# Decoding 64-bit weights: the low word and the sign taken from ScalarE to VectorE, with a new order of steps in the opening

## The chip, the cores and the metric

One core of a Trainium2 chip runs one program. The metric is the device time of that program in microseconds; a lower one is better. TensorE multiplies matrices, VectorE, ScalarE and GpSimd (POOL in the profile) work on elements, SyncE (SP) issues the transfers.

## The reference, cut to what matters

A windowed attention with a linear bias (8 batches, 8 heads, 576 positions, head size 64, window 128) is followed by a gated two-layer block:

```
scores = q k^T / 8 + slope * -(i - j)    where 0 <= i - j < 128
x      = softmax(scores) v                               # 576 x 512 per batch
h      = gelu(x w_in);  u, v = halves of h               # w_in 512 x 1024
v_n    = (v - mean) / sqrt(var + 1e-6) * g_ln
gated  = u * (w_sg v_n + b_sg)                           # w_sg 576 x 576
out    = x + gated w_out                                 # w_out 512 x 512
```

The scale factors that make `w_in` and `w_out` are 64-bit, so these two arrive as 64-bit floats.

## The kernel before

Every large product is made of three matmuls: each operand is split into a high and a low part of TensorE's short format, and high x high, high x low and low x high are added (`mm3`, line 570). The weights therefore have to be split before batch 0 can use them.

**Decode of one block of weights** (`split64`, lines 180 to 200; twelve blocks of 128 x 512: eight of `w_in`, k = 0 to 7, and four of `w_out`, k = 8 to 11; `add_wide`, line 500, makes the steps):
- `i{k}` loads the block into one of four buffers (SP, line 177).
- `d{k}` is three passes of ScalarE. L189 scales the low 32-bit word by 2^-29 and writes the rounded result as 16 bits into the low half of that word. L190 scales the high word by 2^-100 and writes it as a 16-bit float into the other half, so that only the sign is left. L191 writes the absolute value of the high word, rebased, to a temporary.
- `b{k}` shifts the temporary left by 3 bits (VectorE, L193). `+{k}` adds the low word to it as integers (GpSimd, L195). `H{k}` writes the high part (ScalarE, L197). `-{k}` writes the low part, the difference (L199; VectorE for odd k, GpSimd for even k).

**The other steps.** 32 pairs of heads, four per batch, each with: loads q and L; scores a and c, or * for both (TensorE, L252); score minima A, B, C, G with the bias (VectorE, L264 and L270); exponentials e, E, j, f, F (ScalarE, L280); R, the inverse of the sums (VectorE, L291, L292); scalings r, s, S (GpSimd, L296); transposes z, t, T (TensorE, L306, L319); masked copies X and Y (VectorE, L314, L315) and P (ScalarE); V, the values (TensorE, L337 to L345); x, h, k (ScalarE, L358 to L370) and l (GpSimd, L367), which gather the pair's output and split it. Per batch: v and tt (in batch 0 the v sums are cut into w and v steps), u, y and O with Oa are TensorE's sums; vg, tg, ug the gelu; nv..b, p, c, h and vn the normalisation of v (VectorE L594 to L602, GpSimd L599, ScalarE L607, VectorE L610), nt.. and tn the same for the tail of 64 rows, which ends in the tile vA; uc, gm, gh, gl, oa copies, gates and sums. wl, wH, w- and tl, tH, t-, bl, bH, b- load and split `w_sg` and the bias `b_sg`.

**Order.** Each step is registered with its engine, the steps that it follows and the buffers that it takes; the length given there is not used when the program is built. `ORDER`, a list written out by hand of all 1769 steps, is the order in which the steps are emitted; `pin` (line 873) makes the instructions of each engine keep that order, the SP queue too. So each engine works down its own part of the list and waits where a step that it needs has not ended. A y step of batch 0 needs all of vn, tn, w-, t- and b-; its last two matmuls (L722, L723) read vA and the tail of `w_sg`. A u step needs h and l of all four pairs and the low parts of blocks 4 to 7.

Of the kernel before, what the change touches and what calls it, by code (L numbers as in the profile page):

```python
# [908 lines left out]
```

## Time and profile before

| | |
|---|---|
| median of 3 runs | 605.91 us (605.49 to 606.16) |
| profiled execution, first to last instruction (span) | 603.9 us |
| TensorE busy (matmul) | 577.9 us, 96% |
| VectorE busy | 394.0 us, 65% |
| ScalarE busy | 374.9 us, 62% |
| GpSimd busy | 233.4 us, 39% |
| chain that ended last | TensorE 81%, ScalarE 10% of the span |

The table's shares are means over the whole span; the opening, in which the weights are decoded, has other limits than the rest. Of the profiled execution the span is its own time on record; the runs' median lies 2.0 us over it. L12 is line 12 of the kernel; a time in a timeline is counted from the span's start.

### The profile page before, as it was taken

The page shows a single profiled execution, that of the slowest core. Times are in us where ns is not written, and L with a number is a line of the kernel's source. Part 1 is how long each engine was busy: PE and PEld are TensorE (multiplying, and loading weights), DVE is VectorE, ACT ScalarE, POOL GpSimd, SP SyncE. Part 2 cuts the span into 40 slices and gives each one's busy share as a digit, 9 for nine tenths or more (in the row PEclk, how much of TensorE's full clock was granted, in tenths as well). Part 3 has the DMA queues.
Part 4 walks back from the last instruction along what each step waited for, and adds up shares of the span by engine and source line. Part 5 has one row for each costly group of instructions (what it writes and reads, how often), then busy time and mean ns, then how long its engine had stood idle before and what let it go on. Part 6 is the DMA issues. An engine that isn't in the chain of part 4 may idle for free.

```text
span 603.9 us, 16878 instructions
## 1 busy us (share of the span) xinstructions
PE 577.9 (96%) x6760; PEld 538.8 (89%) x6760; DVE 394.0 (65%) x1336; ACT 374.9 (62%) x1057; POOL 233.4 (39%) x248
## 2 busy tenths in 40 slices
...
GB/s 279 197 149 216 35 134 99 43 41 65 115 67 64 100 83 82 65 22 12 108 123 43 76 48 74 92 24 81 80 143 2 3 68 117 64 2 1 1 25 132
DMA packets 34898, 47.92 MB, mean 79 GB/s; under 512 B 2946, under 2 KB 24962, under 8 KB 34820
## 3 DMA queue, kind: packets, MB, share of 16 engines
...
q14 instruction: 25, 0.20, 0.1%
...
## 4 chain that ended last, share of the span: by engine, by line
PE 81%; ACT 10%; DVE 1%; POOL 1%; issue 1%; ACTq 0%
PE bank L574 20%; PE bank L576 20%; PE bank L575 20%; PE bank L252 5%; PE bank L337 5%; PE bank L306 4%; ACT e L280 3%; PE bank L342 2%; ACT wst L189 1%; PE bank L723 1%; PE bank L722 1%; PE bank L658 1%; PE bank L345 1%; PE bank L660 1%; ACT wst L190 1%
## 5 line engine op out<-in xcount | busy, mean ns | idle before, releaser
L280 ACT ACTIVATE e<-e,minima 128x128 f32<-128x128 f32 (+1 forms) x288 | 110.3, 385 | 15.0 <-DVE minima L264 14.5
L296 POOL TENSOR_TENSOR e<-e,rr 128x512 f32<-128x512 f32 (+1 forms) x96 | 75.7, 809 | 113.1 <-DVE rr L292 88.7
L264 DVE CUSTOM_DVE_ANT_0 e<-bank,bias 128x128 f32<-128x128 f32 (+1 forms) x320 | 75.9, 275 | 8.4 <-DVE bank L270 0.5
L599 POOL TENSOR_TENSOR rs<-rs,mhalf 128x1 f32<-128x1 f32 (+1 forms) x40 | 30.6, 769 | 126.1 <-DVE rs L596 126.0
L574 PE MATMUL bank<-ws,vn 128*128 128x288 f32 x256 | 78.0, 305 | 0.1
L574 PE MATMUL bank<-xs,wi 128*128 128x288 f32 x256 | 77.2, 302 | 0.7 <-ACT vg L648 0.7
L574 PE MATMUL bank<-g,wo 128*128 128x288 f32 x256 | 77.7, 303 | 0.0
L575 PE MATMUL bank<-xs,wi 128*128 128x288 f32 x256 | 75.5, 295 | 0.0
L576 PE MATMUL bank<-ws,vn 128*128 128x288 f32 x256 | 75.5, 295 | 0.0
L575 PE MATMUL bank<-g,wo 128*128 128x288 f32 x256 | 75.4, 295 | 0.0
L576 PE MATMUL bank<-g,wo 128*128 128x288 f32 x256 | 75.4, 295 | 0.0
L576 PE MATMUL bank<-xs,wi 128*128 128x288 f32 x256 | 75.4, 294 | 0.0
L575 PE MATMUL bank<-ws,vn 128*128 128x288 f32 x256 | 75.4, 294 | 0.0
L367 POOL TENSOR_TENSOR xs<-xf,xs 128x576 fp32r<-128x576 f32 x32 | 45.4, 1427 | 63.4 <-ACT xs L364 63.3
L270 DVE COPY_PREDICATED bank<-sel,bank 128x256 f32<-128x256 uint8 x128 | 54.0, 422 | 18.7 <-PE bank L252 17.7
L252 PE MATMUL bank<-qk 64*64 64x128 f32 (+2 forms) x1536 | 54.9, 287 | 5.6 <-DMA qk<-qkT 3.3
L314 DVE TENSOR_TENSOR px<-bank,m_own 128x512 f32<-128x512 f32 x64 | 43.7, 683 | 23.3 <-PE bank L306 12.6
L252 PEld LDWEIGHTS bank<-qk 64*64 64x64 f32 x1536 | 50.5, 141 | 8.8 <-DMA qk<-qkT 4.0
L737 POOL TENSOR_TENSOR g<-u,g 128x576 fp32r<-128x576 f32 x32 | 45.0, 1420 | 29.3 <-ACT g L734 29.1
L280 ACT ACTIVATION_READ_ACCUMULATOR e<-e,minima 128x1 f32 x288 | 54.3, 188 | 0.0
L574 PE MATMUL bank<-wi,xs 128*128 128x512 f32 x128 | 51.3, 401 | 2.1 <-DVE minima L264 2.1
L576 PE MATMUL bank<-wi,xs 128*128 128x512 f32 x128 | 50.4, 394 | 0.0
...
## 6 DMA issues: line engine op xcount, KB each, us to landing
...
wst<-w_in SPq DMA_DIRECT2D x8, 512.0 KB, 4.3
...
wst<-w_out SPq DMA_DIRECT2D x4, 512.0 KB, 3.2
...
```

Of the source, the lines that this page charges most:

```text
L252: return lambda: nc.tensor.matmul(banks[j][half[s ^ j], dst * R:(dst + k1 - k0) * R], qk[heads[j], 0, q * R:(q + 1) * R], qk[heads[j], 1, ...
L264: nc.vector.tensor_tensor_reduce(out=dst, in0=src, in1=bs, scale=-1.0 / math.sqrt(D), scalar=3e38, op0=ALU.add, op1=ALU.min, accum_out=acc)
L270: nc.vector.copy_predicated(sv[:, :, 0:P], sels[j][:, 0:2] if t2 == 0 else sels[j][:, 1:3], sv[:, :, P:2 * P])
L280: nc.scalar.activation(x, x, AF.Exp, bias=self.nm[0:n, i:i + 1], scale=-1.0, accum_out=self.sm[0:n, i, 0:1])
L296: nc.gpsimd.tensor_tensor(x, x, self.rr[0:n, i:i + m].rearrange("p (m o) -> p m o", o=1).broadcast_to([n, m, c]), ALU.mult)
L314: nc.vector.tensor_tensor(xv[:, 0], cv, over(m_owns[j], T), ALU.mult)
L367: nc.gpsimd.tensor_tensor(lo_of(self.xs), self.xf, hi_of(self.xs).bitcast(F32), ALU.subtract)
L574: nc.tensor.matmul(dst, ah, bh, start=(first and i == 0), stop=False)
L575: nc.tensor.matmul(dst, ah, bl, start=False, stop=False)
L576: nc.tensor.matmul(dst, al, bh, start=False, stop=(last and i == n - 1))
L599: nc.gpsimd.tensor_tensor(x["rs"][0:rows], x["rs"][0:rows], mhalf[0:rows], ALU.pow)
L737: nc.gpsimd.tensor_tensor(st[f"g{f}"][:, 1, :], st["u"][:, f, :], st[f"g{f}"][:, 0, :].bitcast(F32), ALU.subtract)
```

## The change

ScalarE keeps one pass of the decode step, the absolute value. VectorE gets two new steps for each block: `M{k}` multiplies the low word (an unsigned integer) by 2^-29, adds 2^23 and writes the result as a float in place, whose low bits are then the rounded number; `N{k}` takes the upper 16 bits of the high word, keeps the sign bit alone and writes it over the upper 16 bits of the low word. The shift b now follows N.

```diff
-        low_half = w.bitcast(U16).rearrange("p (n t) -> p n t", t=4)[:, :, 0]
-        sign_half = w.bitcast(F16).rearrange("p (n t) -> p n t", t=4)[:, :, 1]
+        r = w.bitcast(F32).rearrange("p (n t) -> p n t", t=2)[:, :, 0]
+        quarters = w.bitcast(U16).rearrange("p (n t) -> p n t", t=4)
         fi, ri = f.bitcast(I32), w0.bitcast(I32)
 
-        nc.scalar.activation(low_half, w0, AF.Copy, scale=2.0 ** -29)
-        nc.scalar.activation(sign_half, w1f, AF.Copy, scale=2.0 ** -100)
         nc.scalar.activation(f, w1f, AF.Abs, scale=REBASE)
+        yield
+        nc.vector.tensor_scalar(r, w0, 2.0 ** -29, 2.0 ** 23, ALU.mult, ALU.add)
+        yield
+        nc.vector.tensor_scalar(quarters[:, :, 1], quarters[:, :, 3], 0x8000, None, ALU.bitwise_and)
         yield
         nc.vector.tensor_scalar(fi, fi, 3, None, ALU.logical_shift_left)
...
         add(f"d{k}", "ACT", 1.13, at, begin, [f"i{k}"], take=take_f)
-        add(f"b{k}", "DVE", 0.43, at, go, [f"d{k}"], port=True)
+        add(f"M{k}", "DVE", 0.43, at, go, [f"d{k}"], port=True)
+        add(f"N{k}", "DVE", 0.6, at, go, [f"M{k}"], port=True)
+        add(f"b{k}", "DVE", 0.43, at, go, [f"d{k}", f"N{k}"], port=True)
         add(f"+{k}", "POOL", 1.26, at, go, [f"b{k}"])
```

The first 585 steps of `ORDER` get a new order, with the 24 new steps among them; the last 1184 steps stay as they are. The old and the new list, from their start to the first y sums of batch 0:

```
before:
q0 i0 Q0 q1 a0 c0 A0 d0 B0 b0 C0 G0 E0 e0 j0 f0 +0 F0 a1 A1 i4 R0 B1 c1 d4 C1 r0 s0 S0 z0 t0 T0 G1 b4 +4 i1 L0 q2 wl2 wl3 d1 f1
H0 E1 j1 P0 wH2 F1 e1 wH3 a2 c2 b1 X0 Y0 A2 R1 B2 +1 w-2 C2 s1 S1 r1 w-3 -0 V0 t1 T1 z1 G2 X1 i5 q3 i2 i3 q4 wl0 L1 a3 c3 e2 d5
f2 F2 j2 E2 d2 x0 P1 d3 H1 A3 R2 b5 B3 Y1 C3 s2 r2 S2 +5 b3 b2 -1 t2 z2 T2 a4 G3 A4 B4 E3 e3 j3 h0 f3 F3 +2 +3 l0 R3 V1 x1 X2 Y2
c4 w30 s3 r3 L2 H4 h1 H2 w10 z3 t3 wH0 P2 i6 i7 q5 L3 tl l1 V2 C4 w11 w31 G4 w-0 S3 T3 X3 d7 H5 -4 F4 x2 P3 h2 -5 *5 w20 w21 Y3
A5 l2 -2 H3 e4 j4 d6 tH E4 f4 -3 b7 +7 V3 b6 +6 B5 x3 H7 h3 k1 j5 R4 s4 C5 G5 l3 r4 S4 F5 e5 E5 H6 f5 w32 w12 w00 w01 w22 t4 w02
v02 v03 T4 z4 v00 X4 -7 -6 Y4 R5 vg03 v01 P4 vg01 k2 q6 L4 i11 gb i10 L5 wl1 t- s5 bl nv30b nv30p nv10b nv30c nv10p nv10c wH1
d11 nv30h nv10h vn03 k0 vg00 b11 +11 vn01 u020 u001 V4 u031 t5 vg02 k3 x4 d10 u000 uc000 nv00b nv20b X5 nv00c S5 nv00p nv20p r5
nv20c uc020 nv00h nv20h uc031 vn00 b10 +10 i8 q7 i9 vn02 w-1 tt0 z5 u011 T5 u021 u030 tj0 d8 H10 tg0 u010 Y5 nt0b -10 nt0p nt0c
uc021 P5 bH uc030 uc011 H11 -11 uc010 nt0h uc001 V5 d9 ug0 b- tn0 *6 b8 A6 b9 B6 +8 H8 +9 -8 H9 e6 E6 y020 C6 y001
...
after:
q0 a0 A0 B0 E0 q1 a1 A1 Q0 e0 B1 j0 E1 c0 C0 G0 i0 d0 M0 f0 F0 N0 b0 R0 c1 C1 G1 i1 d1 i2 d2 L0 M2 M1 N1 q2 b1 N2 s0 r0 z0 t0 X0
j1 e1 S0 T0 b2 f1 F1 R1 a2 c2 P0 Y0 +0 H0 A2 B2 s1 wl3 r1 wH3 C2 G2 t1 V0 X1 w-3 +1 e2 S1 T1 Y1 j2 x0 h0 -0 q3 z1 a3 P1 c3 l0 F2
A3 f2 E2 q5 R2 s2 S2 B3 C3 G3 +2 r2 e3 wl2 k0 gb L1 L2 q4 V1 wH2 w-2 t2 X2 T2 Y2 j3 f3 F3 E3 R3 s3 z2 x1 a4 A4 c4 H1 i3 d3 P2 h1
H2 V2 x2 h2 B4 j4 e4 E4 r3 -1 M3 C4 N3 G4 b3 t3 X3 l1 S3 T3 Y3 F4 f4 R4 i4 i5 w30 i6 l2 d4 k2 +3 -2 z3 d5 P3 w00 w01 w31 *5 H3
d6 L3 V3 x3 M4 N4 -3 M5 w32 b4 i7 A5 B5 C5 e5 k1 N5 b5 G5 M6 N6 h3 s4 S4 w10 w20 +4 q7 t4 T4 L4 d7 E5 H4 f5 M7 b6 N7 j5 b7 w11
w21 w22 i11 L5 l3 v02 k3 w02 F5 X4 R5 v03 vg03 nv30b r4 +5 H5 -5 -4 q6 w12 v01 +6 H6 +7 d11 H7 -7 nv30c M11 vg01 nv10b nv10c v00
wl1 tl -6 nv30p tt0 wH1 nv30h vn03 u000 N11 b11 vg00 nv00b s5 S5 nv10p nv10h vn01 i10 d10 M10 tH uc000 u031 nv00c vg02 nv20b
nv20c N10 w-1 +11 z4 u021 uc021 t- nv00p nv00h vn00 nv20p nv20h uc031 P4 vn02 bl wl0 wH0 u030 u010 uc030 r5 H11 b10 +10 H10 -10
tj0 Y4 u001 tg0 z5 t5 u020 uc001 bH u011 uc011 uc010 nt0b nt0c -11 uc020 P5 b- nt0p nt0h tn0 V4 T5 x4 i8 d8 ug0 i9 d9 *6 A6 M8
N8 b8 X5 B6 M9 N9 w-0 y010 y020 +8 H8 -8 h4 E6 C6 y031
...
```

## Rows read from the trace of the kernel before

**Rows 1.** Busy time in stretches of 15 us: the stretch and its length in us, then each engine's busy us (and count), the granted TensorE clock as a share of full speed, the DMA share and GB/s.

```profile
0.00:15.00 15.00, 7.76 (x106) 6.28 (x107) 10.87 (x55) 12.90 (x35) 9.80 (x29) 0.99 0.83 279
15.00:30.00 15.00, 11.73 (x177) 9.63 (x177) 11.24 (x51) 14.89 (x43) 9.78 (x9) 0.67 0.63 196
30.00:45.00 15.00, 8.29 (x127) 6.64 (x127) 10.14 (x44) 14.84 (x42) 8.79 (x9) 0.77 0.50 146
45.00:60.00 15.00, 12.22 (x208) 9.70 (x209) 12.13 (x37) 14.80 (x39) 11.07 (x11) 1.00 0.67 217
```

**Rows 2.** The same view for five other stretches, with the same columns.

```profile
0.00:88.10 88.10, 67.12 (x935) 56.10 (x935) 66.17 (x234) 84.81 (x216) 57.44 (x72) 0.90 0.53 169
0.00:90.10 90.10, 68.95 (x946) 57.70 (x946) 68.09 (x236) 86.81 (x219) 57.44 (x72) 0.91 0.53 168
13.50:88.10 74.60, 59.76 (x831) 50.03 (x831) 56.72 (x187) 73.38 (x183) 49.05 (x46) 0.89 0.47 150
88.10:122.70 34.60, 32.91 (x451) 30.96 (x452) 26.81 (x114) 25.33 (x74) 19.59 (x17) 1.00 0.24 73
122.70:604.00 481.30, 477.89 (x5377) 451.79 (x5375) 301.04 (x989) 264.74 (x769) 156.34 (x159) 1.00 0.20 63
```

**Rows 3.** TensorE's timeline from 84.8 to 90.5 us: start, duration in us, engine, line, operation, output and inputs, count, and the idle time before with what ended it. L337 opens V5, L252 is the score step behind it, the first L574 on ws is the first y.

```profile
84.84 1.15 PE L337 MATMUL bank<-px,vt 128*64 128x64 f32 x32
...
86.44 1.58 PE L252 MATMUL bank<-qk 64*64 64x192 f32 x48
88.08 0.40 PE L574 MATMUL bank<-ws,vn 128*128 128x288 f32 x1
...
90.14 0.40 PE L722 MATMUL bank<-wsA,vA 128*128 128x288 f32 x1 [0.21 <-DVE vA L610]
```

**Rows 4.** TensorE's waits from 88 to 126 us, the costliest: line, what it waited for, us in total, times, longest.

```profile
PE bank L306 <- POOL e L296: 1.4, 2, 1.1
```

**Rows 5.** ScalarE's passes of the decode and GpSimd's add, from the view of the tile wst (count, then the shortest, median and longest in ns, first and last start, shapes), and, as the last row, ScalarE's contiguous copy L197 from the view of lines up to 125 us (mean ns).

```profile
L189 ACT ACTIVATE wst<-wst x12: 1321/1353/1399, 6.4 to 89.4; 128x512 uint16<-128x512 uint32 x12
L190 ACT ACTIVATE wst<-wst x12: 1345/1370/1392, 7.7 to 90.8; 128x512 f16<-128x512 f32 x12
L191 ACT ACTIVATE tmp<-wst x12: 691/698/715, 8.8 to 92.0; 128x512 f32<-128x512 f32 x12
L195 POOL TENSOR_TENSOR tmp<-tmp,wst x12: 1282/1304/1614, 10.1 to 93.3; 128x512 int32<-128x512 int32 x12
...
L197 ACT ACTIVATE wi<-tmp 128x512 fp32r<-128x512 f32 x8 | 5.1, 633 | 0.0
```

**Rows 6.** ScalarE's timeline of the first decode step (start, duration, line).

```profile
6.37 1.33 ACT L189 ACTIVATE wst<-wst 128x512 uint16<-128x512 uint32 x1
8.82 0.69 ACT L191 ACTIVATE tmp<-wst 128x512 f32<-128x512 f32 x1
```

**Rows 7.** VectorE's operations up to 90.1 us by line and shape: count, busy us, mean ns of one, idle time before; as the first row, the shift L193 over the whole span (shortest, median, longest ns).

```profile
L193 DVE TENSOR_SCALAR tmp<-tmp x12: 366/426/1503, 9.5 to 92.7; 128x512 int32<-128x512 int32 x12
...
L193 DVE TENSOR_SCALAR tmp<-tmp 128x512 int32<-128x512 int32 x10 | 5.2, 526 | 7.7 <-ACT tmp L191 7.7
L199 DVE TENSOR_TENSOR wi<-tmp,wi 128x512 fp32r<-128x512 f32 x4 | 4.1, 1027 | 0.4 <-ACT wi L197 0.4
L610 DVE SCALAR_TENSOR_TENSOR vn<-vg,rs,vn 128x512 fp32r<-128x512 f32 x4 | 3.0, 748 | 3.0 <-ACT vn L607 3.0
L602 DVE SCALAR_TENSOR_TENSOR vg<-vg,mv,gb 128x512 f32<-128x512 f32 x4 | 2.8, 744 | 0.0
L557 DVE SCALAR_TENSOR_TENSOR wsB<-wsh,bsel,wst 2x576 fp32r<-2x576 f32 x1 | 0.8, 808 | 0.0
L199 DVE TENSOR_TENSOR wo<-tmp,wo 128x512 fp32r<-128x512 f32 x1 | 0.7, 693 | 0.9 <-ACT wo L197 0.9
```

**Rows 8.** The two longest waits of VectorE ahead of its first score minima, from its timeline (in brackets).

```profile
1.39 0.92 DVE L131 CAST own<-rel_i 64x64 f32<-64x64 int32 x1 [0.38 <-POOL rel_i L129]
...
6.26 0.43 DVE L270 COPY_PREDICATED bank<-sel,bank 128x256 f32<-128x256 uint8 x1 [1.12 <-PE bank L252]
```

**Rows 9.** VectorE's timeline from 53 us on, and under it GpSimd's from 48.5 us on.

```profile
53.19 1.29 DVE L199 TENSOR_TENSOR wi<-tmp,wi 128x512 fp32r<-128x512 f32 x1
54.40 1.50 DVE L193 TENSOR_SCALAR tmp<-tmp 128x512 int32<-128x512 int32 x1
...
48.97 1.29 POOL L199 TENSOR_TENSOR wi<-tmp,wi 128x512 fp32r<-128x512 f32 x1
...
52.49 1.44 POOL L367 TENSOR_TENSOR xs<-xf,xs 128x576 fp32r<-128x576 f32 x1 [2.23 <-ACT xs L364]
53.88 1.74 POOL L199 TENSOR_TENSOR wi<-tmp,wi 128x512 fp32r<-128x512 f32 x1
```

**Rows 10.** GpSimd's first scaling of probabilities, from its timeline.

```profile
13.59 1.29 POOL L296 TENSOR_TENSOR e<-e,rr 128x64 f32<-128x64 f32 x2 [2.19 <-DVE rr L292]
```

**Rows 11.** GpSimd's operations up to 88.1 us by line and shape: count, busy us, mean ns, idle time before and what ended it.

```profile
L195 POOL TENSOR_TENSOR tmp<-tmp,wst 128x512 int32<-128x512 int32 x10 | 13.8, 1383 | 16.1 <-DVE tmp L193 10.3 <-ACT wi L197 4.1 <-issue 1.7
L296 POOL TENSOR_TENSOR e<-e,rr 128x512 f32<-128x512 f32 x12 | 12.4, 1039 | 4.2 <-DVE rr L292 3.1 <-ACT ws L537 0.6 <-ACT xf L359 0.5
L199 POOL TENSOR_TENSOR wi<-tmp,wi 128x512 fp32r<-128x512 f32 x4 | 5.6, 1400 | 0.6 <-ACT wi L197 0.6
```

**Rows 12.** The page's list of DMA issues: count, KB each, median us to landing.

```profile
wst<-w_in SPq DMA_DIRECT2D x8, 512.0 KB, 4.3
```

More of the change, by code (lines that the diff above doesn't have):

```diff
@@ new lines, in attention_gmlp @@
+        *10 A10 B10 C10 V9 x9 D01 u130 q11 *11 uc130 X8 tn1 y111 Y8 L8 V8 ug1 f10 A11 x8 E10 G10 e10 F10 B11 E11 e11 j11 h9
+        O031 y100 C11 G11 oa031 j10 R10 y130 y101 y110 s10 l9 t10 y131 gm111 h8 F11 k9 f11 gm130 gm110 X10 R11 r10 z10 P10
+        gh11 S10 T10 Y10 gm101 gm131 gm100 gh10 gh13 s11 y120 y121 gm120 gm121 S11 gl11 gl10 L11 D02 q13 L10 D03 q12 t11 V10
+        gh12 x10 gl12 *12 X11 A12 Oa10 B12 C12 r11 gl13 T11 Y11 z11 O100 O120 O110 oa110 G12 E12 P11 f12 h10 l8 V11 j12 x11
@@ new lines, in attention_gmlp @@
+        k8 h11 F12 e12 *13 A13 oa100 B13 l11 l10 C13 R12 G13 E13 j13 s12 f13 e13 F13 O131 R13 oa131 O111 v21 vg21 nv12b t12
+        v20 oa111 X12 nv12c nv12p s13 vg20 u200 uc200 nv12h k11 nv02b vn21 nv02p S12 r13 r12 Oa11 O101 oa101 nv02c oa120
+        u221 u211 O121 T12 z12 nv02h k10 Y12 uc211 P12 uc221 tt2 L12 q15 D10 q14 L13 V12 D11 vn20 tj2 x12 tg2 *14 nt2b nt2p
+        S13 nt2c A14 oa121 B14 t13 z13 v22 v23 T13 u230 C14 P13 nt2h G14 tn2 X13 vg23 vg22 j14 u220 Y13 nv22b V13 nv22c
+        nv32b nv32c E14 e14 uc220 F14 f14 x13 nv22p nv22h *15 A15 u201 uc201 uc230 R14 O130 oa130 B15 s14 nv32p nv32h S14
@@ new lines, in attention_gmlp @@
+        nv03c vn31 oa210 oa231 P16 uc300 nv03h vn30 tj3 tg3 nt3b nt3c O211 T16 Y16 oa211 v33 v32 u310 O200 nt3p nt3h tn3
+        oa200 r17 z17 uc310 P17 uc330 vg32 vg33 L16 q19 L17 D20 D21 q18 V16 *19 A19 t17 u301 x16 u321 uc321 uc301 nv33b X17
+        B19 C19 G19 f19 F19 nv33c nv33p nv33h j19 E19 T17 Y17 nv23b O230 oa230 nv23c nv23p vn33 u311 u320 O221 uc320 u331
+        oa221 V17 e19 nv23h R19 vn32 x17 h17 uc311 uc331 *18 A18 y320 y330 B18 r19 l17 s19 t19 ug3 C18 G18 gm320 X19 E18 S19
+        h16 f18 F18 j18 e18 y310 gm310 T19 z19 y331 y301 l16 gm330 R18 s18 r18 S18 P19 gm331 Y19 y311 gm311 gh31 gh33 gl31
@@ new lines, in attention_gmlp @@
+        gl33 t18 y321 gm321 gh32 gl32 y300 z18 gm300 gm301 P18 gh30 q21 q20 D22 D23 L19 L18 V19 *20 T18 gl30 X18 A20 O311
+        B20 oa311 Y18 O320 Oa31 O301 C20 G20 oa320 V18 x19 k16 h19 j20 l19 x18 h18 E20 f20 *21 A21 oa301 B21 F20 k19 l18 k17
+        k18 j21 Oa30 O300 O310 C21 oa310 e21 f21 G21 F21 tt4 tj4 tg4 e20 R20 s20 oa300 v41 nt4b nt4c nt4p nt4h tn4 u431 v43
+        u400 uc400 vg41 uc431 vg43 nv14b v42 v40 u421 nv14c nv34b r20 S20 nv14p nv34p nv14h vn41 E21 t20 X20 nv34c vg42
+        nv34h vn43 R21 O321 T20 Y20 vg40 s21 nv04b nv04p r21 u401 z20 oa321 nv24b nv24p P20 u420 u411 uc411 uc420 uc401
@@ new lines, in attention_gmlp @@
+        B25 C25 G25 F24 k22 k20 f25 e24 E24 f24 j25 e25 u500 tt5 j24 R24 oa431 tj5 u511 O411 O400 O401 v52 u520 uc500 tg5
+        nt5b s24 S24 r24 nt5p nt5c nt5h uc511 v51 O410 oa400 t24 z24 tn5 oa401 vg52 vg51 nv15b nv15p nv15c P24 nv15h nv25b
+        oa410 oa411 u510 uc510 nv25p O420 T24 u521 v53 F25 uc521 E25 X24 vn51 nv25c Y24 nv25h vn52 vg53 v50 R25 oa420 s25
+        r25 z25 vg50 P25 L24 D40 L25 nv35b nv05b q27 D42 q26 D41 V24 x24 *27 nv05c A27 nv35c B27 nv35p nv05p S25 e27 uc520
+        t25 u531 u530 nv35h E27 nv05h uc530 T25 X25 Y25 vn53 C27 G27 u501 uc501 uc531 h24 j27 ug5 O430 vn50 f27 V25 *26
@@ new lines, in attention_gmlp @@
+        nv16b nv16c v63 z29 P29 k26 k25 u621 u620 nv16p nv16h u600 t28 vn61 vg63 uc600 O530 oa500 nv26p nv26c nv36b nv36p
+        S29 nv36c nv26h uc601 nv36h X28 vn62 vn63 T28 O510 oa510 tt6 z28 P28 tj6 uc620 u610 t29 u611 T29 u630 Y28 uc621 tg6
+        uc611 nt6b oa530 nt6c nt6p nt6h u631 uc631 uc630 uc610 tn6 D50 L28 V28 L29 D52 q31 q30 L31 x28 ug6 *31 X29 y620 y611
+        Y29 A31 V29 L30 D51 D53 B31 gm620 C31 G31 *30 A30 e31 E31 F31 f31 h28 e30 j31 gm611 B30 R31 E30 j30 C30 G30 y631
+        y610 gm610 gh61 y621 gm621 gh62 x29 f30 F30 s31 l28 S31 r31 y600 z31 t31 X31 gm600 R30 T31 Y31 y601 gl61 gl62 h29
```

107 lines of the change are left out of this document (39 added, 68 removed).

## The prediction

> **What bounds the kernel now.** I read the busy time by stretch first. From 15 to 60 us ScalarE is busy 14.8 to 14.9 of every 15 us, while TensorE has holes: 7.2, 3.3, 6.7 and 2.8 us of idle time in the first four stretches, 20.0 in all [rows 1]. The two long stretches say the same: TensorE is busy 67.1 of the first 88.1 us, 32.9 of the next 34.6 and 477.9 of the last 481.3 [rows 2]. So the kernel is TensorE's work plus 26 us of holes, 21 of them ahead of 88.1 us, and nothing else can be won. [...]
>
> Next I looked at what ends the opening. At 88.08 us TensorE starts y, the first spatial sum of batch 0, and from there it runs almost closed: its waits from 88 to 126 us are 1.4 us for GpSimd and 0.2 for vA [rows 3, 4]. I call 88.1 the **gate**: y needs all weights, their low parts and the normalised v, and its thirteenth matmul waits for vA, the last step of that normalisation [rows 3]. Up to the gate ScalarE is busy 84.8 of 88.1 us, VectorE 66.2, GpSimd 57.4 [rows 2]. ScalarE bounds the opening, with 3.3 us lost. About a third of its time is the two passes that the change takes away: 1.35 and 1.37 us each, against 0.70 for the pass that stays [rows 5].
>
> **The change, part by part.**
>
> *ScalarE.* In one decode step the first pass starts at 6.37 and the third at 8.82 us [rows 6], so a step loses 2.45 us of queue. Eleven such steps start ahead of the gate; ten stay there (the new list moves d8 behind it: 2.45 and the third pass's 0.70, some 3.2 us more). ScalarE's need falls from 84.8 by 24.5 and 3.2 to 57.1 us. It stops being the bound; what is late next must be found on the other engines.
>
> *VectorE.* It gets twice twelve instructions, ten pairs ahead of the gate. M reads and writes every second 32-bit word, N every fourth 16-bit word, 512 elements each. No VectorE row has such a pattern. The lower end is the shift on contiguous words, 0.43 us [rows 7]; the upper end is ScalarE's passes with such a strided write, 1.35 and 1.37 us [rows 5]. A strided read alone costs ScalarE little (0.70 against 0.63 for the contiguous copy) [rows 5]. I take 0.50 for M and 0.60 for N, near the row of the same engine and kind of operation, 1.1 together. By rows alone the pair lies between 0.86 and 2.72. VectorE is busy 68.1 us by 90.1, when vA is done; 2.4 of that are waits inside L193 (526 against 426 ns, ten times) and L199 (1027 against the 693 of a free one, four times) [rows 2, 7]. So 65.7 and 11.0 and 1.5 of waiting ahead of its first score minima [rows 8] make 78.2 us. VectorE alone would be done 12 us earlier than now.
>
> *VectorE and GpSimd together.* The row that decides is another one. L199 on VectorE is issued at 53.19 and takes 1.29 us; it ends 0.55 after GpSimd's L367 ends. GpSimd's L199, issued at 53.88, takes 1.74 and ends 1.14 after VectorE's. VectorE's shift, issued at 54.40, takes 1.50 and ends 0.29 after that [rows 9]. They run one after the other, in turn. Operations of VectorE that only read and write SBUF (L193, L199, L602, L610, L557) and GpSimd's therefore share one resource, and M and N are of that kind. Its need up to the gate, from 13.5 us, when GpSimd begins its steady work [rows 10]:
> - GpSimd: 49.1 busy from 13.5 to 88.1 [rows 2], less 1.2 that was waiting inside L195 and L199 (1383 ns against a median of 1304, ten times; 1400 against 1290, four times) [rows 5, 9, 11], plus 1.3 for the first add, which the new list places after 13.5. 49.1.
> - VectorE as it is: nine shifts of 0.43, five L199 of 0.69, five L602 and five L610 of 0.74, one L557 of 0.81 [rows 7]: 15.5.
> - New: nine pairs of 1.1 (block 0 comes earlier): 9.9.
> - Sum 74.5. Where one takes over from the other, VectorE's operation is 0.14 shorter and GpSimd's 0.15 [rows 7, 9]. Counting that for half of the 43 operations takes off 6.1: 68.4, and the gate could open at 81.9.
>
> No engine gets rid of every hole. I add the 3.3 us that ScalarE lost in the same stretch as the bound: 85.2, that is 2.9 us sooner. The cover of the other 21.6 us that ScalarE gives up is this shared resource.
>
> *The list of steps.* Steps of all engines, also SP's, are moved ahead of the place where both lists agree again. TensorE's list has V5 (1.60 us: 84.84 to 86.44) ahead of the first y now and behind five y sums after [rows 3]. This work does not vanish: 1.6 us of the 2.9 go back. In return some of the 1.6 us of waiting behind the gate can close, since scores and values of pairs 5 to 7 come earlier in ScalarE's list; I count half, 0.8 [rows 3, 4]. On SP, q1 goes ahead of i0, which comes fourth (landing takes 4.3 us [rows 12]), and q5 ahead of q4. The first decode moves behind three exponentials, so i0's lag is hidden; q4's buffer comes free with the scores of pair 2, several steps ahead of pair 4's. I cost these at nothing; if the cover is gone, one landing of 4.3 us falls into the opening. The chain of one block gets 2.45 us shorter on ScalarE and 1.1 longer on VectorE, so no chain gets longer by itself. A wait that the change adds: b waits for M and N, both in VectorE's queue, and behind them stand the score minima, for which the exponentials wait. Behind the common point nothing changes, and TensorE is closed there.
>
> *Sum:* 2.9 - 1.6 + 0.8 = 2.1 us. The profiled execution has a span of 603.9, which becomes 601.8; the runs' median is 605.9, so 2.0 us lie around the span. Forecast **603.8 us**.
>
> **The strided price, weighed.** ScalarE's strided 16-bit write costs 0.65 us over the same pass with a contiguous one [rows 5]. [...]
>
> **Rivals.**
> 1. *The holes grow (no change).* VectorE's queue is in order. Where M, N and b stand behind each other and GpSimd has work, each waits for a GpSimd operation of 1.0 to 1.4 us [rows 11], as the two waits of 1.29 and 1.50 show [rows 9]; nine blocks with two more such waits than I count give the 2.1 us back easily. For it: the resource would be needed 68.4 of 71.7 us, fuller than any but ScalarE now. Against: GpSimd waited 10 of 16 us ahead of L195 for VectorE [rows 11], so VectorE often finds it free. Time 606.
> 2. *Strided operations are dear (slower).* M and N cost half way to ScalarE's strided write, 0.9 each, 1.8 the pair. Place: L193's queue, nine pairs on the shared resource. 9 x 0.7 = 6.3 us more: 610.1. It decides from a pair price of 1.1 + 2.1/9, some 1.33; from 1.47 it is slower by 0.2%. For it: rows 5. Against: the shift's 0.43 shows VectorE faster per element than ScalarE.
> 3. *M, N and GpSimd seldom meet (much faster).* If the list places them where GpSimd waits, VectorE's own need bounds: 78.2 and 3.3 of loss, 81.5 against 90.1, less the 0.8 net of V5 and the waits: 7.8 us, 598.1. For it: the shifts now run unhindered but for one (median 426 ns, longest 1503) [rows 7]. Against: it needs the whole sum of GpSimd and VectorE to overlap, and GpSimd's steps have little room left.
>
> **How the numbers follow.** Forecast (601.5 to 604.7) 0.33; rival 3 0.13; rival 1 0.20; rival 2 0.34, since its condition is open from both sides and the forecast's price is near the lower end. A measurement of this kernel tells some 0.2%, 1.2 us, from no change. So faster 0.46, same 0.20, slower 0.34. The range takes in rival 3 and rival 2 up to a pair price of 1.85: 597.5 to 610.6, with a tenth outside at each end.
>
> **What would show it.** Right: ScalarE busy some 57 us up to the first y, holes in its row; first y at 85 us behind waits on GpSimd or VectorE; M near 0.50 and N near 0.60 where GpSimd rests, and over 1 us where it runs. Wrong: M or N over 0.8 with GpSimd idle (rival 2); first y ahead of 83 (rival 3); first y at 88 or later with short M and N (rival 1); new holes of TensorE behind the gate; the stretch behind the common point longer than before.

## The result, and the profile after

The changed kernel takes 609.78 us (median of 4 runs, 609.54 to 609.79), the kernel before 606.03 (4 runs, 605.49 to 606.19): 1.0065 times as long, 95% interval 1.0052 to 1.0077. It is slower by 3.7 us, where the forecast was 2 us faster. The profiled executions have spans of 607.8 and 603.9 us; the 3.9 between them are explained here.

First the busy time by stretch of the kernel after (length, then busy us and count of TensorE, its weight load, VectorE, ScalarE and GpSimd, granted clock, DMA share, GB/s). It answers to [rows 1, 2].

```profile
15.00:30.00 15.00, 11.10 (x178) 9.62 (x178) 14.36 (x46) 8.11 (x34) 10.48 (x11) 0.70 0.47 160
30.00:45.00 15.00, 10.32 (x205) 8.53 (x206) 14.14 (x61) 12.21 (x47) 10.60 (x10) 1.00 0.62 204
45.00:60.00 15.00, 12.66 (x147) 9.77 (x146) 14.63 (x40) 11.73 (x41) 11.72 (x9) 0.89 0.68 201
60.00:75.00 15.00, 12.39 (x74) 10.62 (x73) 14.72 (x27) 7.36 (x13) 11.29 (x9) 1.00 0.20 68
...
0.00:90.50 90.50, 66.73 (x871) 56.29 (x871) 85.07 (x253) 61.05 (x196) 60.84 (x72) 0.91 0.51 162
90.50:125.00 34.50, 33.51 (x514) 32.05 (x514) 29.78 (x119) 23.72 (x72) 19.65 (x17) 1.00 0.29 89
125.00:608.00 483.00, 479.17 (x5380) 452.25 (x5378) 301.38 (x990) 263.38 (x766) 156.05 (x159) 1.00 0.20 63
```

ScalarE did get its time back: 61.1 us busy up to the gate, against 84.8 of 88.1 [rows 2]. But VectorE now stands where ScalarE stood, busy 14.1 to 14.7 of every 15 us, and TensorE has holes up to the gate: 2.3 and 2.6 us of them in the last two stretches shown. Behind 125 us little is different (TensorE idle 3.8 us where it was 3.4). The granted clock up to the gate is 0.91, and was 0.90 [rows 2].

The gate itself, in TensorE's timeline after (start, duration, line; L254 is the score step, the first L578 on ws the first y, L726 the thirteenth). It answers to [rows 3].

```profile
88.95 1.55 PE L254 MATMUL bank<-qk 64*64 64x128 f32 x48
90.44 0.41 PE L578 MATMUL bank<-ws,vn 128*128 128x288 f32 x1
...
92.13 0.29 PE L726 MATMUL bank<-wsA,vA 128*128 128x288 f32 x1
```

The first y starts at 90.44 us, 2.36 later than before. Behind the gate TensorE is busy 512.7 us (33.51 and 479.17) where it was 510.8 [rows 2], for V5 stands there now, and idle 4.8 where it was 5.1: 1.6 more in all, which with the 2.36 is the difference of the spans.

What led up to it is in the chain that ended last. Of the first 90.4 us of that chain VectorE holds 67 us, 17 of them in M and N. Only from 81.4 us on is it TensorE's own work, and part of that ran at a granted clock of 0.51 of full speed, behind a hole in which TensorE waited for GpSimd's scalings. The rows are the shares of the chain up to 90.5 us by line (L266 and L272 are the score minima with the bias), TensorE's timeline with the hole and two of the matmuls behind it, and the stretch with the clock of 0.51.

```profile
by line: DVE e L266 14.0%; DVE wst L191 10.2%; DVE bank L272 9.1%; DVE wst L193 9.1%; DVE px L317 6.1%; DVE px L316 5.3%; issue 4.8%; DVE tmp L195 4.5%; DVE wi L201 4.1%; DMA qk<-qkT 3.7%; PE bank L254 3.4%; DVE vg L606 3.1%; DVE st L598 2.
...
80.39 0.33 PE L321 MATMUL bank<-ident,e 128*128 128x128 f32 x1 [2.14 <-POOL e L298]
...
82.27 0.44 PE L580 MATMUL bank<-xs,wi 128*128 128x288 f32 x1
82.51 0.44 PE L578 MATMUL bank<-xs,wi 128*128 128x288 f32 x1
...
82.00:85.40 3.40, 3.40 (x17) 3.40 (x16) 3.30 (x6) 3.05 (x7) 2.43 (x2) 0.51 0.24 88
```

From 82.0 to 85.4 us the matmuls start 0.24 us apart, behind that 0.13. Fourteen such steps make an estimate of 1.5 us that the stretch cost, out of the 2.36, in this execution; before, the granted clock was 1.00 from 45 us on. Where the low stretches lay in the other three runs is not recorded, but they took the same time within 0.3 us.

Why VectorE is full is seen in its operations up to 90.5 us by line and shape (count, busy us, mean ns of one, idle before). L191 is M, L193 N, L195 the shift b, L201 the low part, L606 and L614 the normalisation. The rows answer to [rows 7].

```profile
L193 DVE TENSOR_SCALAR wst<-wst 128x512 uint16<-128x512 uint16 x10 | 10.4, 1044 | 0.1
L191 DVE TENSOR_SCALAR wst<-wst 128x512 f32<-128x512 uint32 x10 | 10.0, 1012 | 0.0
L195 DVE TENSOR_SCALAR tmp<-tmp 128x512 int32<-128x512 int32 x10 | 5.4, 541 | 0.0
L201 DVE TENSOR_TENSOR wi<-tmp,wi 128x512 fp32r<-128x512 f32 x4 | 4.0, 1018 | 0.0
L606 DVE SCALAR_TENSOR_TENSOR vg<-vg,mv,gb 128x512 f32<-128x512 f32 x4 | 3.7, 937 | 0.0
L614 DVE SCALAR_TENSOR_TENSOR vn<-vg,rs,vn 128x512 fp32r<-128x512 f32 x4 | 3.3, 836 | 0.3 <-ACT vn L611 0.3
L201 DVE TENSOR_TENSOR wo<-tmp,wo 128x512 fp32r<-128x512 f32 x1 | 2.4, 2414 | 0.0
```

Set against the free durations these are mostly waiting. The view of the tile wst has the shortest, median and longest in ns (then first and last start):

```profile
L191 DVE TENSOR_SCALAR wst<-wst x12: 372/1161/1635, 12.3 to 95.4; 128x512 f32<-128x512 uint32 x12
L193 DVE TENSOR_SCALAR wst<-wst x12: 728/770/1971, 12.8 to 96.7; 128x512 uint16<-128x512 uint16 x12
```

M takes 0.42 us when nothing is in its way (the mean of ten in experiment 1; the shortest here is 0.37) and its median is 1.16; N takes 0.75 (0.74 as the mean of ten in experiment 2) and up to 1.97. Ten M at 1.01 instead of 0.42 are 5.9 us of waiting, ten N 2.9, ten shifts 1.1, L201 3.0 (four at 1.02 and one at 2.41 instead of 0.69), L606 and L614 0.8 and 0.4 (free 0.74): 14.1 us, against the 2.4 of before. The waiting that the change brought, 11.7, is as much as the ten pairs themselves take (1.17 each).

Timelines show three such waits and the price of the first: VectorE's, under it GpSimd's and ScalarE's.

```profile
16.74 1.51 DVE L191 TENSOR_SCALAR wst<-wst 128x512 f32<-128x512 uint32 x1
18.28 0.75 DVE L193 TENSOR_SCALAR wst<-wst 128x512 uint16<-128x512 uint16 x1
...
23.59 0.29 DVE L266 CUSTOM_DVE_ANT_0 e<-bank,bias 128x128 f32<-128x128 f32 x1
...
71.50 1.97 DVE L193 TENSOR_SCALAR wst<-wst 128x512 uint16<-128x512 uint16 x1
...
86.48 2.41 DVE L201 TENSOR_TENSOR wo<-tmp,wo 128x512 fp32r<-128x512 f32 x1
...
14.25 2.29 POOL L298 TENSOR_TENSOR e<-e,rr 128x512 f32<-128x512 f32 x3 [5.83 <-DVE rr L294]
16.49 1.47 POOL L197 TENSOR_TENSOR tmp<-tmp,wst 128x512 int32<-128x512 int32 x1
...
71.30 1.55 POOL L542 TENSOR_TENSOR ws<-wst,ws 128x576 fp32r<-128x576 f32 x1
...
86.94 1.41 POOL L542 TENSOR_TENSOR ws<-wst,ws 128x576 fp32r<-128x576 f32 x1
...
23.98 0.40 ACT L282 ACTIVATE e<-e,minima 128x128 f32<-128x128 f32 x1 [4.79 <-DVE minima L266]
```

An M issued at 16.74 ends at 18.25, 0.29 after GpSimd's add (16.49 to 17.96). N ends 0.62 after L542 (71.30 to 72.85), L201 0.54 after another (86.94 to 88.35). Meanwhile the score minima queue behind M, N, b and the masked copies; ScalarE, freed by the change, idles 4.79 us for them at 23.98. In the view of waits up to the gate (us in total, times, longest) this has become the large item of ScalarE, and the wait for the inverses of the sums that of GpSimd (5.3 us before):

```profile
POOL e L298 <- DVE rr L294: 13.2, 4, 5.8
ACT e L282 <- DVE minima L266: 12.0, 8, 4.8
```

### The profile page after: what moved, and what is told of

The parts are those of the page before. It is cut to its first block, busy times and chain, and to the rows that moved or that the text cites. A ratio compares the mean times of both kernels' runs of the same rounds, so it can differ in the third digit from the quotient of the medians.

```text
span 607.8 us, 16878 instructions
## 1 busy us (share of the span) xinstructions
PE 579.4 (95%) x6760; PEld 540.6 (89%) x6760; DVE 416.2 (68%) x1360; ACT 348.2 (57%) x1033; POOL 236.5 (39%) x248
## 4 chain that ended last, share of the span: by engine, by line
PE 82%; DVE 13%; ACT 2%; POOL 2%; issue 1%; DMA 1%; DVEq 0%; POOLq 0%
PE bank L578 20%; PE bank L580 20%; PE bank L579 20%; PE bank L254 6%; PE bank L339 5%; PE bank L308 4%; DVE e L266 2%; PE bank L344 2%; DVE wst L191 2%; DVE bank L272 1%; PE bank L727 1%; DVE wst L193 1%; PE bank L726 1%; PE bank L347 1%; PE bank L662 1%; PE bank L664 1%
## 5 line engine op out<-in xcount | busy, mean ns | idle before, releaser
L298 POOL TENSOR_TENSOR e<-e,rr 128x512 f32<-128x512 f32 (+1 forms) x96 | 78.1, 833 | 123.9 <-DVE rr L294 122.8
L266 DVE CUSTOM_DVE_ANT_0 e<-bank,bias 128x128 f32<-128x128 f32 (+1 forms) x320 | 76.0, 275 | 7.9
L603 POOL TENSOR_TENSOR rs<-rs,mhalf 128x1 f32<-128x1 f32 (+1 forms) x40 | 31.6, 791 | 126.3 <-DVE rs L600 126.2
L578 PE MATMUL bank<-xs,wi 128*128 128x288 f32 x256 | 78.1, 305 | 2.5 <-ACT vg L652 1.9
L578 PE MATMUL bank<-ws,vn 128*128 128x288 f32 x256 | 77.9, 304 | 0.0
L578 PE MATMUL bank<-g,wo 128*128 128x288 f32 x256 | 77.6, 303 | 0.0
L580 PE MATMUL bank<-xs,wi 128*128 128x288 f32 x256 | 76.2, 298 | 0.6 <-DVE wi L201 0.6
L579 PE MATMUL bank<-xs,wi 128*128 128x288 f32 x256 | 76.2, 298 | 0.0
L272 DVE COPY_PREDICATED bank<-sel,bank 128x256 f32<-128x256 uint8 x128 | 54.1, 423 | 18.2 <-PE bank L254 17.4
L254 PE MATMUL bank<-qk 64*64 64x128 f32 (+2 forms) x1536 | 53.7, 286 | 1.7 <-DMA qk<-qkT 1.6
L254 PEld LDWEIGHTS bank<-qk 64*64 64x64 f32 x1536 | 49.8, 141 | 4.6 <-DMA qk<-qkT 2.2
L578 PEld LDWEIGHTS bank<-xs,wi 128*128 128x128 f32 x256 | 48.8, 190 | 4.5 <-ACT vg L652 2.4
L578 PE MATMUL bank<-wi,xs 128*128 128x512 f32 x128 | 51.7, 404 | 0.0
```

Of the source, the lines that this page charges most:

```text
L254: return lambda: nc.tensor.matmul(banks[j][half[s ^ j], dst * R:(dst + k1 - k0) * R], qk[heads[j], 0, q * R:(q + 1) * R], qk[heads[j], 1, ...
L266: nc.vector.tensor_tensor_reduce(out=dst, in0=src, in1=bs, scale=-1.0 / math.sqrt(D), scalar=3e38, op0=ALU.add, op1=ALU.min, accum_out=acc)
L272: nc.vector.copy_predicated(sv[:, :, 0:P], sels[j][:, 0:2] if t2 == 0 else sels[j][:, 1:3], sv[:, :, P:2 * P])
L298: nc.gpsimd.tensor_tensor(x, x, self.rr[0:n, i:i + m].rearrange("p (m o) -> p m o", o=1).broadcast_to([n, m, c]), ALU.mult)
L578: nc.tensor.matmul(dst, ah, bh, start=(first and i == 0), stop=False)
L579: nc.tensor.matmul(dst, ah, bl, start=False, stop=False)
```

## The experiments

All have the kernel before run beside them; its medians were 605.98, 605.92, 605.67, 605.58 and 605.69 us in the five groups. Ratios are to it, with 95% intervals. "Old list" is `ORDER` of before, "new list" that of the change. The theories: **turns** (VectorE's operations on SBUF and GpSimd's run one after the other, as L199 with 1.29 us and the shift with 1.50 did in [rows 9], and the new list puts M and N where GpSimd works), **load** (VectorE has too much work, wherever it stands), **order** (the list itself). The first four ran as one group, the next four as the second.

**1. Old list, new decode.**

```diff
 # ORDER of before, and in it, for each k:
-b{k}
+M{k} N{k} b{k}
```

> The old list of steps with the new decode: M and N stand right ahead of b, and nothing else is moved. Turns (VectorE's SBUF operations and GpSimd's run one after the other, and the new list puts M and N where GpSimd has work): in the old list VectorE and GpSimd both waited for the decode at this place, so M and N meet little; ScalarE's need ahead of the first y falls by some 25 us, the waits inside VectorE's instructions stay under 6 us, first y near 84 us, 601 to 604 us. Load (VectorE's 11.7 us of added work are enough, with or without waits): first y at 90 us as after the change, 608 to 610. Order (the new list itself is worse): 606 or less, VectorE's waits tell nothing.

Measured 604.37 us (603.86 to 605.29), 0.9976 [0.9966, 0.9987]; first y at 87.89 in the profiled execution, the slowest of the eight. The first y came later than the 84 expected by turns; the time fits turns, and order too (606 or less), and rules out load by itself. With the same decode the old list is 5.4 us faster than the new one. In its rows up to 88 us M is free (mean 418 ns of ten) and only N waits:

```profile
L193 DVE TENSOR_SCALAR wst<-wst 128x512 uint16<-128x512 uint16 x10 | 10.2, 1022 | 0.3
L191 DVE TENSOR_SCALAR wst<-wst 128x512 f32<-128x512 uint32 x10 | 4.2, 418 | 0.0
```

Waits inside VectorE's operations are 3.7 us (N 2.7, b 0.3, L201 0.7) where the new list has 14.1. VectorE holds 36 us of the chain up to the first y, against 67 with the new list. The decode moved off ScalarE is worth 1.6 us by itself, and the new list takes it away.

**2. Old list, the sign alone on VectorE.**

```diff
+        nc.scalar.activation(low_half, w0, AF.Copy, scale=2.0 ** -29)
         nc.scalar.activation(f, w1f, AF.Abs, scale=REBASE)
         yield
-        nc.vector.tensor_scalar(r, w0, 2.0 ** -29, 2.0 ** 23, ALU.mult, ALU.add)
-        yield
         nc.vector.tensor_scalar(quarters[:, :, 1], quarters[:, :, 3], 0x8000, None, ALU.bitwise_and)
 # ORDER of before, N{k} ahead of b{k}
```

> The old list, half of the decode moved: only the sign's AND goes to VectorE, right ahead of b; the rounding stays on ScalarE. Turns: ScalarE's need ahead of the first y falls by some 11 us, VectorE's rises by 7.5, few waits; first y near 85 us, 602 to 605. Load: half of the loss of the whole change, 607 to 608. Order: no more than 606.

Measured 598.13 us (597.77 to 598.34), 0.9871 [0.9856, 0.9886]: 7.8 us faster than before, and the fastest kernel of this study that computes all of the reference. This is more than turns (602 to 605) or load (607 to 608) had expected; only order's 606 or less holds. The first y comes at 81.55. Its stretches, its N (L192) and shift (L194), and ScalarE's waits for the minima:

```profile
15.00:30.00 15.00, 9.75 (x175) 7.76 (x174) 14.25 (x52) 13.62 (x49) 10.51 (x10) 1.00 0.68 228
30.00:45.00 15.00, 11.30 (x198) 8.90 (x199) 14.12 (x56) 13.11 (x39) 11.47 (x12) 0.89 0.65 184
45.00:60.00 15.00, 14.32 (x164) 11.08 (x163) 13.21 (x40) 13.83 (x51) 12.51 (x11) 1.00 0.60 187
```

```profile
L192 DVE TENSOR_SCALAR wst<-wst 128x512 uint16<-128x512 uint16 x10 | 7.4, 741 | 0.0
L194 DVE TENSOR_SCALAR tmp<-tmp 128x512 int32<-128x512 int32 x10 | 6.5, 652 | 0.0
```

```profile
ACT e L281 <- DVE minima L265: 3.0, 4, 1.2
```

VectorE and ScalarE are both near full, N does not wait up to the first y (the shift behind it does, 652 ns against a free 426), and TensorE is nearly closed from 45 us on. Of the amounts tried with the old list (none, one or two passes) one is the best.

**3. New list, old decode.**

```diff
-        nc.vector.tensor_scalar(r, w0, 2.0 ** -29, 2.0 ** 23, ALU.mult, ALU.add)
-        nc.vector.tensor_scalar(quarters[:, :, 1], quarters[:, :, 3], 0x8000, None, ALU.bitwise_and)
+        nc.scalar.activation(low_half, w0, AF.Copy, scale=2.0 ** -29)
+        nc.scalar.activation(sign_half, w1f, AF.Copy, scale=2.0 ** -100)
```

> The new list with the old decode on ScalarE; M and N issue nothing. Turns: VectorE's waits fall back to some 3 us, ScalarE bounds again with 82 to 85 us of need, and V5 stands behind the gate: first y at 88 to 90 us, 606 to 609. Load: VectorE is free of the added work, first y at 88, 606. Order: the list costs the same whatever is decoded where: 609 to 611.

Measured 618.01 us (617.74 to 618.75), 1.0201 [1.0187, 1.0215]; first y at 97.92. All three theories had ended at 611 or below: a miss. The new list needs a light ScalarE: with the old decode ScalarE is busy 14.8 and 14.9 of 15 us between 45 and 75 us, VectorE 7.1 and 7.0. The list is fitted to the new decode, and still worse with it than the old list.

**4. New list, M and N without turns.** In place of M and N stand sums over a constant tile of about the same length; GpSimd's add takes the high word, so the weights' low word and sign are left out of the result.

```diff
-        nc.vector.tensor_scalar(r, w0, 2.0 ** -29, 2.0 ** 23, ALU.mult, ALU.add)
+        nc.vector.tensor_reduce(out=idle[:, 0:1], in_=<bias, 256>, axis=X, op=ALU.add)
         yield
-        nc.vector.tensor_scalar(quarters[:, :, 1], quarters[:, :, 3], 0x8000, None, ALU.bitwise_and)
+        nc.vector.tensor_reduce(out=idle[:, 0:2], in_=<bias, 2 x 256>, axis=X, op=ALU.add)
```

> [...] Turns: VectorE has the same work, but it no longer takes turns with GpSimd for it: waits inside VectorE's instructions ahead of the first y fall from 14 us to under 6, first y at 82 to 86 us, 602 to 606. Load: first y stays at 90 us, 609 to 610. Order: 609 to 610.

Measured 602.96 us (602.88 to 603.07), 0.9951 [0.9939, 0.9963]; first y at 83.65, 6.8 ahead of the kernel after, and the time is 6.8 shorter. The sums (L192, L194) took their 0.41 and 0.68 us (0.42 and 0.69 at most) with GpSimd busy 59.5 of the 83.65 us, and some of the waiting falls on the shift (L196) and the normalisation (L607) instead:

```profile
L194 DVE TENSOR_REDUCE idle<-bias 128x2 f32<-128x512 f32 x10 | 6.8, 681 | 0.1
L196 DVE TENSOR_SCALAR tmp<-tmp 128x512 int32<-128x512 int32 x10 | 6.7, 671 | 0.0
L607 DVE SCALAR_TENSOR_TENSOR vg<-vg,mv,gb 128x512 f32<-128x512 f32 x4 | 4.6, 1150 | 0.0
...
L192 DVE TENSOR_REDUCE idle<-bias 128x1 f32<-128x256 f32 x10 | 4.1, 406 | 0.1
```

The waits inside VectorE come to 7.0 us, half of those of the kernel after (the shift 2.5, L607 1.6, L202 2.6, L615 0.3; turns had expected under 6), so with the same work 7 us of waits less gave 6.8 us of time, of which the low clock stretch of the kernel after may be 1.5. In the new list the turns of M and N alone turn the sign of the change.

**5. New list without M and N.** Both lines taken out, GpSimd's add on the high word.

> The new list without M and N; GpSimd's add takes the high word in place of the low one, so low word and sign are left out. It shows what the change could give if its work on VectorE cost nothing. Turns: against the run with the reductions (603.0) only VectorE's 11 us of work fall away, against the change the waits too; first y at 75 to 80 us, 594 to 599. Load: the same. If the list or TensorE's own steps held it (order): 602 or more.

Measured 596.49 us (595.47 to 596.99), 0.9842 [0.9829, 0.9856]; first y at 79.29. Against experiment 4 the same work of 1.1 us per block, free of turns of its own, costs 6.5 us. So both count under the new list: 6.8 for the turns, 6.5 for the load. The turns of the other operations do not go: here the shift, the low part and the normalisation wait 9.4 us in all up to 80 us, most of it in the shift (L193, free 0.43) and L604 (free 0.74).

```profile
L193 DVE TENSOR_SCALAR tmp<-tmp 128x512 int32<-128x512 int32 x10 | 8.3, 838 | 0.0
L604 DVE SCALAR_TENSOR_TENSOR vg<-vg,mv,gb 128x512 f32<-128x512 f32 x4 | 4.9, 1229 | 0.0
```

**6. Old list, the rounding alone on VectorE.** M stands just ahead of d; the sign stays on ScalarE, behind the absolute value, and after M.

```diff
+        nc.vector.tensor_scalar(r, w0, 2.0 ** -29, 2.0 ** 23, ALU.mult, ALU.add)
+        yield
         nc.scalar.activation(f, w1f, AF.Abs, scale=REBASE)
+        nc.scalar.activation(sign_half, w1f, AF.Copy, scale=2.0 ** -100)
```

> The old list, the other half of the decode moved: the rounding goes to VectorE just ahead of the ScalarE step, the sign stays on ScalarE behind it. Turns: a free M was 0.42 us against 1.36 of ScalarE, a free N 0.75 against 1.10, so this half is the cheaper one: ScalarE's need ahead of the first y falls by 13 us, VectorE's rises by 4, one operation fewer to wait for GpSimd than in the whole change; first y at 79 to 83 us, 596 to 600. Load: less work on VectorE than with the sign alone (598.1), so also 596 to 600. Against both: M stands in VectorE's queue ahead of the decode and waits for the block's transfer or a GpSimd operation, score minima behind it are late, 601 to 605.

Measured 608.67 us (608.08 to 610.11), 1.0050 [1.0038, 1.0063]; first y at 93.00. I had expected 596 to 600, or 601 to 605 with M late: a miss of both, by a wait of its own. ScalarE's sign pass (L192) needs M, which stands behind minima and copies in VectorE's queue, and everything else of ScalarE stands behind the sign pass:

```profile
ACT wst L192 <- DVE wst L189: 16.9, 7, 4.2
```

So this is no measure of the rounding's price; it shows what a short step costs when another engine's queue stands on it.

**7. Old list, M ahead of d and N ahead of b.**

```diff
-M{k} N{k} b{k}
+M{k} ahead of d{k}, N{k} ahead of b{k}
```

> The old list, the whole new decode, but M stands ahead of the ScalarE step and N ahead of b, so that they aren't back to back. Turns: M, N and b no longer wait behind each other for GpSimd three times in a row; 600 to 604, a little under the 604.4 with M and N together. Load: VectorE has the same work, 604 to 605.

Measured 603.53 us, 0.9965 [0.9952, 0.9978]; first y at 87.07. Not to be told from experiment 1 (0.9976): whether M stands right ahead of N and b or ahead of d makes no difference here. Its waits inside VectorE are 5.8 us, 2.1 more than in experiment 1.

**8. New list, the sign alone on VectorE.** The decode of experiment 2 with the new list, M taken out of it.

> The new list with the rounding on ScalarE and the sign on VectorE. Between the new list's 609.8 (both on VectorE) and 618.0 (none) when the list is what costs and is fitted to a light ScalarE: 608 to 614. If turns alone made the loss and the list costs nothing: 598 to 602 as with the old list.

Measured 605.30 us, 0.9992 [0.9983, 1.0001]; first y at 87.44. It lies between the two expectations (608 to 614, 598 to 602). The new list costs 7.2 us against the old one with this decode too, and the waits inside VectorE are 12.2 us where experiment 2 has 3.2.

**9 to 11. Is it M's load or ScalarE's relief?** In the old list the decode with both passes moved gives 604.4 and with the sign alone 598.1, though the second has more on ScalarE. Four kernels with the old list and N on VectorE settle what the rounding costs on either engine. Experiment 9 is experiment 1 with a sum over a constant tile in M's place, 10 is experiment 2 with such a sum ahead of each N, 11 is experiment 2 without the rounding pass.

```diff
 # 9 (from 1)
-        nc.vector.tensor_scalar(r, w0, 2.0 ** -29, 2.0 ** 23, ALU.mult, ALU.add)
+        nc.vector.tensor_reduce(out=idle[:, 0:1], in_=<bias, 256>, axis=X, op=ALU.add)
 # 10 (from 2)
+        nc.vector.tensor_reduce(out=idle[:, 0:1], in_=<bias, 256>, axis=X, op=ALU.add)
 # 11 (from 2)
-        nc.scalar.activation(low_half, w0, AF.Copy, scale=2.0 ** -29)
```

> The old list with M and N ahead of each b, as in the kernel that gave 604.37 us, but in place of M stands a sum over a constant tile of the same length (0.41 us), an operation that GpSimd did not delay in the earlier run; the low word is left out of the result and GpSimd's add takes the high word instead. N is as it was. Turns: M's cost over the kernel with the sign alone (598.13 us) is mostly its turns with GpSimd, so this comes to 598 to 600.5, and ScalarE's waits for the score minima fall from 16.0 us to under 9. Load: twelve operations of 0.4 us more in a queue that is already the fullest cost the same wherever they read from: 602 to 604.5, and the waits for the minima stay over 12 us.

> The old list, the rounding on ScalarE and the sign on VectorE (the kernel of 598.13 us), and ahead of each N the sum over a constant tile of 0.41 us, which does no work for the result. In the old list with the whole decode moved, M took its free 0.42 us (mean 418 ns of ten), so its turns with GpSimd can't be what that kernel (604.37) lost to this one; what is left is M's load in VectorE's queue, or that a lighter ScalarE lets other work come at the wrong time. Load: 602.5 to 605, since VectorE gets the 4.2 us of M at a place where exponentials wait behind it. A lighter ScalarE: 598 to 600.5.

> The old list with the sign alone on VectorE, and no rounding anywhere: the low word is left out of the result, and GpSimd's add takes the high word. The fourth of the four kernels with and without the pass of ScalarE and with and without a step of 0.41 us on VectorE. Load: without M the waits for the minima fall from 16.3 us to under 8, and it comes at or under the kernel with the pass on ScalarE: 594 to 598. A lighter ScalarE at the wrong time: 601 to 604.

| old list, N on VectorE | no step in M's place | 0.41 us in M's place |
|---|---|---|
| rounding on ScalarE | 598.13 (0.9871 [0.9856, 0.9886]) | 604.37 (0.9981 [0.9970, 0.9993]) |
| no rounding on ScalarE | 599.90 (0.9905 [0.9890, 0.9920]) | 604.14 (0.9972 [0.9963, 0.9982]) |

Read across, twelve steps of 0.41 us on VectorE, none of which took over 0.42, cost 6.2 and 4.2 us. Nor do they lengthen the turns of the others: N waits more and the shift less, and all waits inside VectorE are 3.2 and 3.4 us in the upper row, 3.5 and 3.1 in the lower. N and the shift in experiment 10 (L195, L197) and in 11 (L192, L194):

```profile
L195 DVE TENSOR_SCALAR wst<-wst 128x512 uint16<-128x512 uint16 x10 | 10.3, 1035 | 0.0
L197 DVE TENSOR_SCALAR tmp<-tmp 128x512 int32<-128x512 int32 x10 | 4.6, 461 | 0.0
```

```profile
L194 DVE TENSOR_SCALAR tmp<-tmp 128x512 int32<-128x512 int32 x10 | 7.5, 748 | 0.0
L192 DVE TENSOR_SCALAR wst<-wst 128x512 uint16<-128x512 uint16 x10 | 7.4, 738 | 0.0
```

Read down, twelve passes of 1.36 us off ScalarE bring nothing: 1.8 us longer without the step, 0.2 shorter with it, the second not to be told from none. Experiment 9's turns were a miss, and had to be: M had been free in experiment 1. Experiment 11 came out above its 594 to 598 too. The reason stands in the stretch from 15 to 45 us, here of experiment 10 and then of 11:

```profile
15.00:45.00 30.00, 21.45 (x310) 17.12 (x308) 28.55 (x105) 25.07 (x82) 20.23 (x20) 0.89 0.61 193
```

```profile
15.00:45.00 30.00, 22.96 (x326) 18.23 (x328) 28.47 (x109) 21.34 (x77) 22.44 (x21) 0.89 0.63 203
```

VectorE is busy 28.5 of 30 us with or without the rounding on ScalarE (28.4 in experiment 2). It is the bound as soon as N is there, and ScalarE's relief finds no taker. The granted clock in that stretch was 0.94 in experiment 2, 0.89 in 10 and 11, 0.70 in 9, but it does not make the differences: over its four runs experiment 2 had 0.983 to 0.997 for the whole span and took 597.8 to 598.3 us, and the run of experiment 9 with 0.994 took 604.15, as the median of all ten.

**12. Experiment 2 with VectorE relieved.** GpSimd writes the low part of the odd blocks too.

```diff
-        add(f"-{k}", "DVE", 0.62, at, go, [f"H{k}"], port=True)     # odd k
+        add(f"-{k}", "POOL", 1.26, at, go, [f"H{k}"])               # all k
```

> The kernel of 598.13 us (old list, the sign alone on VectorE), with the low part of every block written by GpSimd; before, VectorE wrote that of the odd blocks. VectorE loses five operations ahead of the first y, 4.4 us with their waits; GpSimd, busy 58.3 of 81.6 us there, gets five of 1.3 us, 6.5 in all. VectorE's load decides: in the old list 4.2 us of steps on VectorE cost 4.2 and 6.2 us of time, so 4.4 us less give back 2 to 4: 594 to 596. Shared resource: GpSimd and VectorE take turns in SBUF, and its need grows by 6.5 less 3.5, so the time grows by up to 3: 598 to 601.

Measured 599.26 us (598.60 to 600.34), 0.9892 [0.9875, 0.9908], against 0.9871 of experiment 2, the intervals overlapping: the gain of 2 to 4 us did not come. VectorE's rows up to 82.5 us say where it went (L192 is N, L194 the shift):

```profile
L192 DVE TENSOR_SCALAR wst<-wst 128x512 uint16<-128x512 uint16 x10 | 9.9, 994 | 0.0
L194 DVE TENSOR_SCALAR tmp<-tmp 128x512 int32<-128x512 int32 x10 | 7.5, 748 | 0.0
```

Five operations less, but N rose from 741 to 994 ns and the shift from 652 to 748: 3.5 of the 4.4 us came back as waiting for GpSimd. VectorE's time here is its work and its turns, and GpSimd's work counts in the second.

## Why the prediction was wrong

**What held.** ScalarE's relief: 57 us were forecast up to the gate and 61.0 measured (58.7 of the first 88.1), from 84.8. The prices: M 0.50 and N 0.60 were taken; they are 0.42 and 0.75, 1.17 for the pair instead of 1.1, and free ones in a row start 0.45 and 0.56 us apart. So rival 2 fell, although its sign came true. M's every second 32-bit word ran in 0.42 us, as the shift's contiguous words did in 0.43 [rows 7]; only N's 16-bit steps lie above that, at 0.75. The shared resource: M and N take turns with GpSimd (up to 1.64 and 1.97 us), as [rows 9] had let expect.

**The step that failed** is the loss on the shared resource, put at 3.3 us, and with it the new order, costed at nothing. I had worked out the resource's need up to the gate as 68.4 us and added 3.3, the loss of ScalarE in the same stretch: the gate at 85.2. It came at 90.44, so the loss was 8.5 by that sum, of which the dearer pair explains 0.6 and the stretch of TensorE at the clock of 0.51, by the estimate above, 1.5. The experiments part the miss. With the old list the change gave 1.6 us (experiment 1), where the sum without its terms for the list (V5 and the credit) has 2.9: 1.3 short. The new list costs 5.4 us, where the sum had 0.8 net for it: 4.6 more. So the larger part of the miss came with the order, whose waits on the shared resource the sum did not hold.

ScalarE's 3.3 was the wrong likeness. Its passes hardly vary in length (L189 1321 to 1399 ns [rows 5]), so it rarely waited inside an operation. VectorE, taking turns with GpSimd, stood still inside its operations, as in the M of 1.51 us at 16.74, and with it all that stood behind in its queue: the minima for ScalarE's exponentials (12.0 us of waits), the sums' inverses for GpSimd's own scalings (13.2), the masked copies for TensorE (1.2). So the 14.1 us of waits are no idle time that something else fills, they lengthen VectorE's work. Halving them by experiment 4 gave 6.8 of time. They are no price one for one, though: experiment 5 has 9.4 us of them and is the fastest of all, as VectorE has less to do there, and experiment 7 has 2.1 more than experiment 1 and is no slower.

Behind it stands a second error, in "VectorE alone would be done 12 us earlier". That sum (78.2) holds no turns, and the turns took the room: VectorE was busy 85.0 of the 90.4 us up to the gate. Experiments 9 to 11 show that from 15 to 45 us N alone fills it (28.4 and 28.5 of 30 us busy without M), and that 4.9 us more of steps cost 4 to 6 us, even without one turn of their own. So the rounding should have stayed on ScalarE. The room can be read per stretch: in [rows 1] VectorE is busy 11.2, 10.1 and 12.1 of 15 us from 15 to 60 us, which leaves 11.5 us. The new list put six pairs there, which take 7.0 us when free and took 12.3.

**The list.** It costs 5.4 us with this decode (experiment 1) and 7.2 with the sign alone (experiment 8). The waits inside VectorE are 14.1 us with it, 3.7 without: it sets M, N and b of several blocks behind each other where GpSimd adds and scales, as the timelines at 16 us show. No row of before could show that. That these waits are all that the list costs is not shown: in experiment 3, with M and N absent, they are 5.3 us, and the list costs 12. I gave rival 1 ("each waits for a GpSimd operation of 1.0 to 1.4 us") 0.20 with two more such waits per block as price. That is the mechanism that ran; the waits were 11.7 us instead of the few that would have closed the gain, so the result was slower and not equal. The sign given for it, a first y at 88 or later with short M and N, came true in its first half alone: seven of the ten M and four of the ten N up to the gate were long, each beside an operation of GpSimd.

**Behind the gate** V5 came back as forecast, a little dearer: 1.9 us more of TensorE's busy time instead of 1.6. Of the credit of 0.8 for waits only 0.3 came: TensorE's idle time is 1.0 us in the 34.5 behind the gate, against 1.7 [rows 2], but 0.4 more than before behind that. In the terms of the sum: gate 2.4 later instead of 2.9 sooner, V5 1.9, credit 0.3, together 4.0 slower.
